# Attention and a maxout feed-forward on one core: regrouping the half-array matmuls of two pairs of heads into one turn

## The chip, the cores and the metric

The kernel runs on one core of one Trainium2 chip. The metric is the time of one execution on the device, in microseconds (us); the time shown for a kernel is the median of several executions. A profile is taken of one further execution; its span runs from the first to the last instruction on the core, and a little time lies around it.

## The reference: what is computed

Eight batches, twelve heads, sequence 448, head dimension 64. Attention with a softmax that has one more term in its denominator, then a feed-forward block whose hidden layer is the largest of three projections:

```python
scores = (1 / sqrt(64)) * q @ k.T                    # per batch and head: 448 x 448
e = exp(scores - m)                                  # m: row maximum
attn = e / (sum(e) + exp(-m) + 1e-09)                # the same as exp(s) / (sum(exp(s)) + 1)
x = (attn @ v), heads side by side                   # 3584 tokens x 768
h = max(max(x @ w1, x @ w2), x @ w3)                 # 768 -> 768
out = h @ w_out                                      # 768 -> 768, float32
```

## The kernel before, in words

**Pairs and engines.** Heads are handled two at a time: a *pair* p is two heads, six pairs make a batch, 48 pairs in all (NP = 48, NPAIR = 6). The sequence of 448 keys is cut into three chunks of 128 and a last one of 64. Matmul inputs are fp16. TensorE (PE) does all products; ScalarE (ACT) does the exponentials and the reciprocals (as Ln, L298, and Exp of minus it, L299); VectorE (DVE) casts q and k, normalizes, and empties the accumulators of the feed-forward part; GpSimd (POOL) scales v into fp16 (`scale_v`); SyncE (SP) issues the loads, the DMA transposes of q and k, and the stores.

**What is done for a pair.** `cast_qk` (L178 to L189) turns the loaded q and k into fp16 on DVE; `transposes` puts them head dimension first, from pair 12 (P_DMA) on by a DMA transpose on SP's queue (L209). `scores(p, c)` (L239) multiplies chunk c of the keys with all queries, one matmul for each head. The contraction is only 64 long, so each of these two matmuls uses one half of the array (64*128 in the profile) and the two run side by side. `exp_scores` (L249) takes both heads in one ACT instruction. `scores_last` (L255) does the last 64 keys of both heads in one matmul over the full array, and `exp_last` (L265) its Exp. `av_main(p, hh)` (L273) multiplies the three chunks of one head with v, with columns of ones beside v, so that the sums of the softmax come out of the same accumulator: three full-array matmuls. `av_last` (L285) adds the last 64 keys, one half-array matmul for each head. `reciprocals` does two Ln (one for each head) and one Exp on ACT, and `normalize(p, hh)` (L307) multiplies on DVE and so writes the input xT of the feed-forward part.

**Accumulators.** All of PSUM is given out: `ps_s` has two tiles of two banks for scores, `ps_av` two banks, one for each head of a pair (tag av), and `ps_u` two banks for the groups. A new tile takes the place of the one two before it in its pool, and its first matmul waits until that one has been read for the last time: by the Exp for scores, by `normalize` for av, by the eviction on DVE for a group.

**Groups.** The feed-forward part of a finished batch is cut into *groups*, kept in a queue and put between the steps of the next pairs to fill PE's time. An up group (L356) is six matmuls of 448 columns, evicted by DVE at L370 (first of three projections) or L372 (maximum with the others). An out group (op, L390) is six matmuls of 384 columns, evicted at L400; two of them fill a row tile, which is then stored. A batch has 18 up groups and then 6 or 8 out groups. `batch_done(b)` puts them in the queue when the last pair of the batch is normalized, and `n_groups` spreads them over the turns, leaving four (LEFT) for the start of the next batch.

**The order around the change.** The order on each engine is written out by hand (`manual_schedule`): every engine takes its instructions in the order of the program. One iteration `it` of the main loop holds the scores of pair `it` and the attention products of the pair before (`prev`). From pair 7 on:

```python
for c in range(2): exp_scores(p, c, scores(p, c))      # half array
group()
avs = [av_main(prev, hh) for hh in range(2)]           # full array
av_last(prev, avs)                                     # half array
stp = scores(p, 2)                                     # half array
stl = scores_last(p)                                   # full array
rb = reciprocals(prev, avs); exp_scores(p, 2, stp); exp_last(p, stl)
group(); normalize(prev, 0, avs, rb)
group(); normalize(prev, 1, avs, rb)
for _ in range(n_groups - 3): group()
```

From iteration 11 on the casts and the transpose of pair it + 2 and the scaling of v of pair it + 1 stand ahead of this, and the loads of pair it + 5 behind it. A run of half-array matmuls between full-array ones is called a stretch below; an iteration has two of them.

Of the kernel before, what the change touches and what calls it, by code (L numbers as in the profile page):

```python
# [21 lines left out]
def kernel(  # L22
# [20 lines left out]
    NPAIR = H // 2  # L43
    NP = B * NPAIR
# [79 lines left out]
    P_DMA = 2 * NPAIR  # L124
# [26 lines left out]
    qkTs = {}  # L151
# [13 lines left out]
    def cast_qk(p):  # L165
        qt, kt, _ = raw[(p // HB) % NRAW]
        h0 = 2 * (p % HB)
        hs = slice(h0, h0 + 2)
        k6, q6 = k16[p % NK], q16[p % NK]
        if p == 0:  # L170

            nc.scalar.copy(out=k6[:, 0:NB], in_=kt[:, hs, 0:NB].rearrange("p h c d -> p c h d"))
            for eng, cs in ((nc.scalar.copy, slice(0, 2)), (nc.vector.tensor_copy, slice(2, NB + 1))):
                eng(out=q6[:, cs], in_=qt[:, hs, cs].rearrange("p h c d -> p c h d"))
        else:
            if p >= P_DMA and (p // NPAIR) % 2:

                nc.vector.tensor_copy(  # L178
                    out=q6[:, 1 : NB + 1], in_=qt[:, hs, 0:NB].rearrange("p h c d -> p c h d")
                )  # L180
                nc.vector.tensor_copy(out=q6[64:128, 0], in_=qt[0:64, hs, NB])
            else:
                nc.vector.tensor_copy(out=q6, in_=qt[:, hs].rearrange("p h c d -> p c h d"))
            nc.vector.tensor_copy(  # L184
                out=k6[:, 0:NB], in_=kt[:, hs, 0:NB].rearrange("p h c d -> p c h d")
            )
        for hh, half in enumerate(halves):
            last = nc.gpsimd if p == 0 else nc.vector
            last.tensor_copy(out=k6[half, NB, hh], in_=kt[0:64, h0 + hh, NB])  # L189

    def scale_v(p):
        vt = raw[(p // HB) % NRAW][2]
        h0 = 2 * (p % HB)
        hs = slice(h0, h0 + 2)
        vs = vst[:, p % VB]
        scaled(
            vs[:, 0 : 2 * NB, D : 2 * D].rearrange("p (h c) d -> p h c d", h=2),
            vt[:, hs, 0:NB],
        )
        for hh, half in enumerate(halves):  # L200
            out_v = vlast[half, p % VB, hh] if p < NPAIR else vs[half, 2 * NB, D : 2 * D]
            scaled(out_v, vt[0:64, h0 + hh, NB])
# [32 lines left out]
    def scores(p, c):  # L235
        qkT, q0, k0 = qkTs[p]
        stp = ps_s.tile([128, 2, 512], FP32, tag="s", name="stp")
        for hh in range(2):
            nc.tensor.matmul(  # L239
                out=stp[:, hh, 0:S],  # L240
                lhsT=qkT[hh * D : hh * D + D, k0 + c * 128 : k0 + c * 128 + 128],
                rhs=qkT[hh * D : hh * D + D, q0 : q0 + S],
                start=True,
                stop=True,
            )
        return stp

    def exp_scores(p, c, stp):
        nc.scalar.activation(out=eT[:, p % 2, c], in_=stp[:, :, 0:S], func=AF.Exp, scale=scale)  # L249

    def scores_last(p):

        stl = ps_s.tile([128, 2, 512], FP32, tag="s", name="stl")
        qkT, q0, k0 = qkTs.pop(p)
        nc.tensor.matmul(  # L255
            out=stl[:, 0, 0:S],
            lhsT=qkT[:, k0 + NB * 128 : k0 + NB * 128 + 128],
            rhs=qkT[:, q0 : q0 + S],
            start=True,
            stop=True,  # L260
        )
        return stl
# [166 lines left out]
    def group():  # L429
        if queue:  # L430
            queue.pop(0)()

    LEFT = 4
    keep_busy(13)
    casts(0)
    transposes(0)
    keep_busy(3)
    for it in range(NP + 1):
        p = it if it < NP else None
        prev = it - 1 if it > 0 else None  # L440
        to_next = NPAIR - it % NPAIR
        n_groups = -(-max(len(queue) - LEFT, 0) // to_next) if it % NPAIR else 4
        n_groups = max(3, min(5, n_groups))

        first = {3: 1, 4: 2}.get(it)
        if first is not None:
            hs = slice(2 * first, 2 * first + 2)
            nc.vector.memset(raw[2][0][64:128, hs, NB - 1 : NB + 1, :], 0.0)
            if first == 1:
                load(NPAIR, 1, "v")  # L450
            load(NPAIR + first, 1)
        if it in (3, 4):
            load_weight(0, it - 3)
        if it in (5, 6, 8):
            load_weight((5, 6, 8).index(it) + 1)
        if it < NPAIR:

            casts(it + 1)
            for c in range(2):
                exp_scores(p, c, scores(p, c))  # L460
            if prev is None:
                keep_busy(3)
                exp_scores(p, 2, scores(p, 2))
                transposes(1)
                exp_last(p, scores_last(p))
            else:
                den, av = (ps_av.tile([128, 512], FP32, tag="av", name=n) for n in ("den", "av"))
                sums_main(prev, den, 1)
                stp = scores(p, 2)
                sums_main(prev, av, 0)  # L470
                stl = scores_last(p)
                sums_last(prev, den, 1)
                sums_last(prev, av, 0)
                exp_scores(p, 2, stp)
                exp_last(p, stl)
                rb = reciprocals_one(den)
                transposes(it + 1)
            if it < NPAIR - 1:
                keep_busy(3)
            else:  # L480

                ups = [up_open()]
                up_part(ups[0], 0, 0, 0, range(3))
                av5 = ps_s.tile([128, 2, 512], FP32, tag="s", name="av5")
                sums_main(p, av5[:, 1], 1)
                sums_main(p, av5[:, 0], 0)
                sums_last(p, av5[:, 1], 1)
                sums_last(p, av5[:, 0], 0)
                rb5 = reciprocals_one(av5[:, 1])
            if prev is not None:  # L490
                normalize_one(prev, av, rb)
            if it == NPAIR - 1:
                normalize_one(p, av5[:, 0], rb5)
                batch_done(0)
        elif it == NPAIR:
            exp_scores(p, 0, scores(p, 0))

            up_part(ups[0], 0, 0, 0, (3,))
            ups.append(up_open())
            up_part(ups[1], 0, 0, 1, range(4))  # L500
            ups.append(up_open(ps_av, "av"))
            up_part(ups[2], 0, 0, 2, range(4))
            for dc in (4, 5):
                for fc, ps in enumerate(ups):
                    up_part(ps, 0, 0, fc, (dc,))
                    if dc == 5:
                        up_close(ps, 0, 0, fc)
            del queue[0:3]
            exp_scores(p, 1, scores(p, 1))
            group()  # L510
            casts(it + 1)
            exp_scores(p, 2, scores(p, 2))
            exp_last(p, scores_last(p))
            group()
            transposes(it + 1)
            group()
        else:
            late = it + 1 < P_DMA
            if not late:

                if it + 2 < NP:
                    cast_qk(it + 2)
                    transposes(it + 2)
                if it + 1 < NP:
                    scale_v(it + 1)
            if p is not None:
                for c in range(2):
                    exp_scores(p, c, scores(p, c))
            group()
            if late:  # L530
                casts(it + 1)
            avs = [av_main(prev, hh) for hh in range(2)]
            av_last(prev, avs)
            if p is not None:
                stp = scores(p, 2)
                stl = scores_last(p)
            rb = reciprocals(prev, avs)
            if p is not None:
                exp_scores(p, 2, stp)
                exp_last(p, stl)  # L540
            if late:
                transposes(it + 1)
            group()
            normalize(prev, 0, avs, rb)
            group()
            normalize(prev, 1, avs, rb)
            if it % NPAIR == 0:
                batch_done(prev // NPAIR)
            if it + 2 == P_DMA:
                cast_qk(it + 2)  # L550
                transposes(it + 2)
            for _ in range(n_groups - 3):
                group()

        for n in range(NPAIR + HB, 2 * NPAIR) if it == NPAIR else (it + 5,):
            if it >= NPAIR and n < NP:
                load(n, 1)
    while queue:
        group()


# [1 line left out]
_INS = ['q', 'k', 'v', 'moe_w1', 'moe_w2', 'moe_w3', 'moe_w_out']  # L563
# [26 lines left out]
```

## Time and profile before

| | us |
|---|---|
| median of 3 executions | 368.15 (368.03 to 368.56) |
| the profiled execution | 367.77 |
| its span | 366.0 |
| PE busy / DVE busy / ACT busy | 357.3 / 243.7 / 220.6 |
| mean granted clock of TensorE | 0.996 |

How to read it. A row of the timeline gives the start and the length of some instructions merged into one, the engine, the line of the kernel, the operation, the tile written and the tiles read, the shape, and how many. Where the engine was idle before, the idle time and what ended it stand in brackets. PEld are the weight loads, which run beside the matmuls of PE. The length of a matmul is longer than its share of PE's time, since the next starts before it has ended; what a matmul costs is the distance from its start to the next one's start. L numbers are lines of the kernel before; up to L251 and from there to L420 the changed kernel has the same ones.

### The profile page before, as it was taken

To read this page: it belongs to the slowest core of one execution; us is meant where nothing else is said; L and a number is where in the kernel's file an instruction comes from. 1 tells how busy PE (TensorE), PEld (TensorE's weight loads), DVE (VectorE), ACT (ScalarE), POOL (GpSimd) and SP (SyncE) were. 2 spreads that over 40 slices of the span, in tenths; PEclk is the share of its full clock that TensorE was granted. 3 is DMA by queue.
4 is the path that set the end of the run, shared out by engine and by line. 5 is a ranking of instruction groups with operands and counts; after the bars stand their busy time and mean duration, and the time that the engine had idled before them with its cause. 6 is when DMAs were issued, how large, how long until landed. Compare 5 with 4: busy or idle time off the path is not lost.

```text
span 366.0 us, 6114 instructions
## 1 busy us (share of the span) xinstructions
PE 357.3 (98%) x2086; PEld 163.7 (45%) x2086; DVE 243.7 (67%) x521; ACT 220.6 (60%) x334; POOL 54.0 (15%) x159
## 2 busy tenths in 40 slices
PE   8999999999999999999999999999999999999994
PEld 3434444444444444444444444444444444445552
DVE  4564777876578677577657867757676876655553
ACT  4986476765666766666566676666566766651000
POOL 4263112211211211211121121121112112000000
PEclk9999999999999999999999999999999999999998
DMA  5999997668877879939764887847775673004006
GB/s 151 228 238 231 232 243 194 167 174 214 169 183 174 209 186 131 220 101 199 181 167 119 179 213 177 159 124 211 172 174 131 162 203 84 0 7 125 2 0 172
DMA packets 87792, 58.61 MB, mean 160 GB/s; under 512 B 43473, under 2 KB 84177, under 8 KB 87761
## 3 DMA queue, kind: packets, MB, share of 16 engines
q1 hardware_dynamic: 83552, 53.27, 60.7%
q0 software_dynamic: 3920, 4.72, 7.4%
q8 instruction: 16, 0.26, 0.3%
q10 hardware_dynamic: 288, 0.23, 0.2%
q14 instruction: 16, 0.12, 0.1%
HBM read 42.47 MB, written 11.01 MB: 146 GB/s over the span
## 4 chain that ended last, share of the span: by engine, by line
PE 94%; DVE 2%; ACT 1%; DMA 1%; issue 0%; SPq 0%; DVEq 0%
PE up L356 45%; PE op L390 15%; PE av L273 13%; PE stp L239 9%; PE stl L255 4%; PE av L285 3%; PE av L316 1%; DMA qin<-in_q_dram 1%; ACT eT L249 1%; PE trT L226 1%; PE trT L221 1%; DVE qkT L233 1%; DVE o_sb L400 0%; PE av L325 0%; PE busy L349 0%
## 5 line engine op out<-in xcount | busy, mean ns | idle before, releaser
L356 PE MATMUL up<-xT,w 128*128 128x448 f16 x864 | 175.3, 353 | 0.7 <-DVE xT L307 0.4
L249 ACT ACTIVATE eT<-stp 128x896 f16<-128x896 f32 x144 | 125.5, 910 | 53.9 <-PE stp L239 53.8
L356 PEld LDWEIGHTS <-w 128*128 128x128 f16 x864 | 81.6, 98 | 81.7 <-issue 12.5
L372 DVE TENSOR_TENSOR hT<-hT,up 128x448 f16<-128x448 f16 x96 | 59.6, 621 | 52.0 <-PE up L356 51.1
L157 POOL TENSOR_SCALAR vst<-vin 128x384 f16<-128x384 f32 x132 | 43.2, 338 | 255.1 <-issue 173.6
L298 ACT ACTIVATE lnd<-av 64x448 f32<-64x448 f32 x84 | 45.2, 538 | 48.9 <-PE av L285 47.9
L390 PE MATMUL op<-w,hT 128*128 128x384 f16 x336 | 59.3, 327 | 0.0
L273 PE MATMUL av<-eT,vst 128*128 128x448 f16 x252 | 54.5, 353 | 0.0
L307 DVE TENSOR_TENSOR xT<-av,rb 64x448 f16<-64x448 f32 x84 | 51.8, 617 | 1.4
L239 PE MATMUL stp<-qkT 64*128 64x448 f16 x288 | 44.1, 353 | 1.5 <-DVE qkT L233 0.7
L370 DVE CAST hT<-up 128x448 f16<-128x448 f32 x48 | 29.8, 624 | 22.9 <-PE up L356 22.2
L400 DVE TENSOR_SCALAR o_sb<-op 128x384 f32<-128x384 f32 x56 | 31.0, 553 | 20.0 <-PE op L390 19.0
L390 PEld LDWEIGHTS <-hT 128*128 128x128 f16 x336 | 31.6, 98 | 24.7 <-issue 4.0
L273 PEld LDWEIGHTS <-vst 128*128 128x128 f16 x252 | 24.6, 98 | 22.5
L184 DVE CAST qk<-kin 128x384 f16<-128x384 f32 x47 | 25.8, 549 | 1.8 <-DMA kin<-in_k_dram 1.4
L265 ACT ACTIVATE eL<-stl 128x448 f16<-128x448 f32 x48 | 25.9, 539 | 0.0
L299 ACT ACTIVATE rb<-lnd 128x448 f32<-128x448 f32 x42 | 24.2, 576 | 1.3
L239 PEld LDWEIGHTS <-qkT 64*128 64x128 f16 x288 | 11.0, 94 | 23.2 <-issue 16.8
L189 DVE CAST qk<-kin 64x64 f16<-64x64 f32 x94 | 17.9, 191 | 1.3
L255 PE MATMUL stl<-qkT 128*128 128x448 f16 x48 | 17.4, 363 | 0.0
L285 PE MATMUL av<-eL,vst 64*128 64x448 f16 x84 | 15.3, 360 | 0.0
L233 DVE COPY qkT<-trT 128x960 f16<-128x960 f16 x11 | 7.2, 656 | 9.9 <-PE trT L226 9.9
(49 smaller groups left out, 110.0 us busy)
## 6 DMA issues: line engine op xcount, KB each, us to landing
out_dram<-o_sb SPq DMA_DIRECT2D x56, 192.0 KB, 2.7
qin<-in_q_dram SPq DMA_DIRECT2D x46, 128.0 KB, 3.0
kin<-in_k_dram SPq DMA_DIRECT2D x45, 128.0 KB, 2.9
vin<-in_v_dram SPq DMA_DIRECT2D x44, 128.0 KB, 3.0
kin<-in_k_dram SPq DMA_DIRECT2D x46, 96.0 KB, 2.7
qin<-in_q_dram SPq DMA_DIRECT2D x45, 96.0 KB, 2.7
vin<-in_v_dram SPq DMA_DIRECT2D x44, 96.0 KB, 2.9
w<-in_moe_w_dram POOLq DMA_DIRECT2D x2, 1152.0 KB, 17.2
```

The lines of the kernel that those rows point to most:

```text
L157: nc.gpsimd.tensor_scalar(out=out, in0=in_, scalar1=LAMBDA, scalar2=1.0, op0=ALU.mult, op1=ALU.mult)
L239: nc.tensor.matmul(out=stp[:, hh, 0:S], lhsT=qkT[hh * D : hh * D + D, k0 + c * 128 : k0 + c * 128 + 128], rhs=qkT[hh * D : hh * D + D, q0 ...
L249: nc.scalar.activation(out=eT[:, p % 2, c], in_=stp[:, :, 0:S], func=AF.Exp, scale=scale)
L255: nc.tensor.matmul(out=stl[:, 0, 0:S], lhsT=qkT[:, k0 + NB * 128 : k0 + NB * 128 + 128], rhs=qkT[:, q0 : q0 + S], start=True, stop=True,)
L273: nc.tensor.matmul(out=av[:, 0:S], lhsT=vst[:, p % VB, hh * NB + c, (1 - hh) * D : (3 - hh) * D], rhs=eT[:, p % 2, c, hh, :], start=(c == ...
L298: nc.scalar.activation(out=lnd[mine], in_=avs[hh][other, 0:S], func=AF.Ln, bias=1.0)
L307: nc.vector.tensor_tensor(out=xTs[b][mine, j, :], in0=avs[hh][mine, 0:S], in1=rb[mine], op=ALU.mult)
L356: nc.tensor.matmul(out=ps[:, 0:S], lhsT=w_sb[i][:, dc, ts(fc, 128)], rhs=xTs[b][:, dc, :], start=(dc == 0), stop=(dc == NDC - 1),)
L370: nc.vector.tensor_copy(out=h, in_=ps[:, 0:S])
L372: nc.vector.tensor_tensor(out=h, in0=h, in1=ps[:, 0:S], op=ALU.max)
L390: nc.tensor.matmul(out=ps[:, 0:NW], lhsT=hTs[sb][:, fc, ts(t, 128)], rhs=wout_sb[:, fc, ts(nh, NW)], start=(fc == 0), stop=(fc == NFC - 1),)
L400: nc.vector.tensor_scalar(out=o_sb[:, ts(nh, NW)], in0=ps[:, 0:NW], scalar1=1.0 / LAMBDA, scalar2=None, op0=ALU.mult,)
```

## The change

From pair 12 on, the loop over single pairs is replaced by a loop whose turn holds two pairs, p and p + 1. The old loop ends at iteration 11, and av_main of pair 11 follows it. In a turn the half-array matmuls stand in three stretches: scores 0 and 1 of p with av_last of p - 1; score 2 of p with score 0 of p + 1; scores 1 and 2 of p + 1 with av_last of p. `scores_last` and `av_main` stand apart from them, among the groups. av_main of p + 1 stands at the end of the turn, behind `finish` of p. A turn takes eight groups where a batch begins and otherwise at least six, as many as share out what is queued. `prepare` (casts, transpose, scaling of v) and `load_next` come twice in a turn, for one pair each. The sizes of the pools stay. The rest of the diff names what was there before.

```diff
     def scores_last(p):
         stl = ps_s.tile([128, 2, 512], FP32, tag="s", name="stl")
-        qkT, q0, k0 = qkTs.pop(p)
+        qkT, q0, k0 = qkTs[p]
...
+    def prepare(p):
+        if p < NP:
+            cast_qk(p)
+            transposes(p)
+        if p - 1 < NP:
+            scale_v(p - 1)
+
+    def load_next(p):
+        if p < NP:
+            load(p, 1)
...
-    for it in range(NP + 1):
-        p = it if it < NP else None
+    for it in range(P_DMA):
+        p = it
...
+    def finish(prev, avs, rb, between=0):
+        for _ in range(between):
+            group()
+        normalize(prev, 0, avs, rb)
+        group()
+        normalize(prev, 1, avs, rb)
+        if prev % NPAIR == NPAIR - 1:
+            batch_done(prev // NPAIR)
+
+    avs = [av_main(P_DMA - 1, hh) for hh in range(2)]
+    for p in range(P_DMA, NP, 2):
+        left = max(len(queue) - LEFT, 0)
+        to_next = (NPAIR - p % NPAIR) // 2
+        n_groups = 8 if p % NPAIR == 0 else max(6, -(-left // to_next))
+        prepare(p + 2)
+        stps = [scores(p, c) for c in range(2)]
+        av_last(p - 1, avs)
+        for c in range(2):
+            exp_scores(p, c, stps[c])
+        group()
+        exp_last(p, scores_last(p))
+        rb = reciprocals(p - 1, avs)
+        finish(p - 1, avs, rb, 1)
+        stps = [scores(p, 2), scores(p + 1, 0)]
+        exp_scores(p, 2, stps[0])
+        exp_scores(p + 1, 0, stps[1])
+        prepare(p + 3)
+        load_next(p + 5)
+        for _ in range(n_groups - 7):
+            group()
+        avs = [av_main(p, hh) for hh in range(2)]
+        stps = [scores(p + 1, c) for c in (1, 2)]
+        av_last(p, avs)
+        for c in (1, 2):
+            exp_scores(p + 1, c, stps[c - 1])
+        rb = reciprocals(p, avs)
+        group()
+        exp_last(p + 1, scores_last(p + 1))
+        finish(p, avs, rb, 2)
+        load_next(p + 6)
+        avs = [av_main(p + 1, hh) for hh in range(2)]
+    av_last(NP - 1, avs)
+    rb = reciprocals(NP - 1, avs)
+    finish(NP - 1, avs, rb, 2)
     while queue:
         group()
```

More of the change, by code (lines that the diff above doesn't have):

```diff
@@ L519 @@
             if not late:
[L521 to L528, printed above, removed]
+                prepare(it + 2)
+            for c in range(2):
+                exp_scores(p, c, scores(p, c))
             group()
@@ L533 @@
             av_last(prev, avs)
-            if p is not None:
-                stp = scores(p, 2)
-                stl = scores_last(p)
+            stp = scores(p, 2)
+            stl = scores_last(p)
             rb = reciprocals(prev, avs)
-            if p is not None:
-                exp_scores(p, 2, stp)
-                exp_last(p, stl)
+            exp_scores(p, 2, stp)
+            exp_last(p, stl)
             if late:
@@ L546 @@
             normalize(prev, 1, avs, rb)
-            if it % NPAIR == 0:
-                batch_done(prev // NPAIR)
             if it + 2 == P_DMA:
@@ L557 @@
                 load(n, 1)
+    def finish(prev, avs, rb, between=0):
[14 more added lines that the diff above has]
+        av_last(p - 1, avs)
+        for c in range(2):
+            exp_scores(p, c, stps[c])
[24 more added lines that the diff above has]
+    finish(NP - 1, avs, rb, 2)
     while queue:
```

## The prediction

> **What bounds the kernel now.** I read the page's totals first, then the chain that ended last, then a stretch of steady turns by engine, then the waits of PE, and last the timeline around one turn.
>
> ```profile
> span 366.0 us, 6114 instructions
> PE 357.3 (98%) x2086; PEld 163.7 (45%) x2086; DVE 243.7 (67%) x521; ACT 220.6 (60%) x334; POOL 54.0 (15%) x159
> PE 94%; DVE 2%; ACT 1%; DMA 1%; issue 0%; SPq 0%; DVEq 0%
> ```
>
> PE sets the time. From 85 to 300 us it is busy for 215.00 of 215.00 us at clock 1.00, and its waits after 80 us add up to one line of 0.4 us:
>
> ```profile
> 85.00:300.00 215.00, 215.00 (x1222) 97.14 (x1221) 152.60 (x326) 140.76 (x214) 28.46 (x90) 1.00 0.74 174
> PE up L356 <- DVE xT L307: 0.4, 1, 0.4
> ```
>
> So a nanosecond of PE order saved is saved from the end, and a new wait of PE is paid in full: there is no slack to absorb it. The timeline of PE over one turn (start, length, line, instructions merged):
>
> ```profile
> 172.33 0.55 PE L239 MATMUL stp<-qkT 64*128 64x448 f16 x4
> 172.81 1.31 PE L356 MATMUL up<-xT,w 128*128 128x448 f16 x6
> 173.96 1.30 PE L273 MATMUL av<-eT,vst 128*128 128x448 f16 x6
> 175.19 0.36 PE L285 MATMUL av<-eL,vst 64*128 64x448 f16 x2
> 175.39 0.35 PE L239 MATMUL stp<-qkT 64*128 64x448 f16 x2
> 175.68 0.36 PE L255 MATMUL stl<-qkT 128*128 128x448 f16 x1
> ```
>
> Lengths overlap, so read start to start. Six full matmuls (64*128 is a half array, 128*128 a full one) go by in 1.15 us, 0.19 each. Six full ones ahead of a half pair take 173.96 to 175.19, 1.23: entering a stretch costs 0.09. Half pair to half pair is 0.20 (175.19 to 175.39); half pair to full is 0.29 (175.39 to 175.68): leaving costs 0.09. **One stretch costs 0.18 us** beyond its own matmuls. The op group that starts at 195.09 hands over at 196.07: 0.98 us, 0.163 each.
>
> **The saving.** Before, pairs 12 to 47 have two stretches each and the last iteration one: 73. After, 18 turns have three and the tail one: 55. Eighteen go: 18 x 0.18 = **-3.3 us**. Matmul counts are unchanged. (The Trainium skill, "TensorE: Matmul & The Clock Gate", section Back-to-back issue gap with the phases ahead of it, lets the drain of one matmul hide under the next; by it a removed stretch saves nothing and the sum is 3.3 us higher. "TensorEngine Tiling (Array Packing)", Key Properties, says that a change of mode drains the array; the steps of 0.29 beside 0.20 side with that page.)
>
> **The new wait.** Before, av_main(prev) comes after the next pair's first scores and a whole group, so the two av banks were freed long before. After, it stands at the end of the turn, directly behind `finish`: group, group, normalize 0, group, normalize 1, av_main(p+1). ps_av has two banks, both still hold pair p, and the changed program's order makes the first weight load of head 1 wait for DVE's normalize 1, which DVE can only start once it has evicted the third group. Before shows exactly this DVE chain, with nobody waiting on it:
>
> ```profile
> 167.69 4.70 PE L356 MATMUL up<-xT,w 128*128 128x448 f16 x24
> 169.03 0.62 DVE L370 CAST hT<-up 128x448 f16<-128x448 f32 x1 [2.05 <-PE up L356]
> 169.57 0.60 DVE L307 TENSOR_TENSOR xT<-av,rb 64x448 f16<-64x448 f32 x1
> 170.17 0.62 DVE L370 CAST hT<-up 128x448 f16<-128x448 f32 x1
> 170.82 0.63 DVE L307 TENSOR_TENSOR xT<-av,rb 64x448 f16<-64x448 f32 x1
> ```
>
> Call S the start of a group's last matmul. The second group there has S = 167.69 + 11 x 0.19 = 169.78; its eviction starts at S + 0.39, and normalize 1 ends at 171.45, S + 1.67. A weight load that waits for DVE starts 0.05 later and its matmul 0.06 (copy ending 23.42, load and matmul below):
>
> ```profile
> 22.76 0.66 DVE L233 COPY qkT<-trT 128x960 f16<-128x960 f16 x1 [0.32 <-PE trT L226]
> 23.47 0.11 PEld L239 LDWEIGHTS <-qkT 64*128 64x128 f16 x4 [0.62 <-DVE qkT L233]
> ```
>
> So head 1 starts at S + 1.73. Unhindered it would start at S + 0.19 + 3 x 0.19 = S + 0.76: **0.97 us lost per turn** (part may show at head 0, which needs normalize 0 and the same DVE). Behind op groups the same reading (groups from 197.99, S = 199.79, normalize 1 from 200.74 for 0.63) gives S + 1.64 against S + 0.73: 0.91. Everything on PE is queued behind that load: head 1, the next stretch, all groups. Each batch has two turns ending in up groups and one in op groups: 12 x 0.97 + 6 x 0.91 = 17.1. The same happens once more where the old loop hands over: av_main(11) follows normalize 1 of pair 10 with no group between (the queue leaves three there): + 0.9. Sum **+18.0**. By the quickest rows (eviction to normalize 0.48) it is about 0.8 each, 15; by the slowest (0.66, and normalize 0 pushing the third eviction by 0.15) about 1.2, 22. I take the chain as it stands.
>
> **The other av_main**, for pair p, has stretch B and n_groups - 7 groups between. Normalize 1 of p-1 waits there for the reciprocals: from the stretch's start, second Exp 1.22 (two take 172.74 to 174.47, overlapping), eL 2.05, two Ln and rb ending near 4.3 (steps 0.56, 0.57, 0.58), then normalize 0, an eviction and normalize 1, over at 6.1 to 6.3. Head 1 is due, from the same start: 0.68 for the stretch (0.20 + 0.20 + 0.28), a group, 0.20 for stl, two groups, 0.09 to enter stretch B, 0.48 for its two pairs, one group, three matmuls 0.57. With groups of 1.14 that is 6.58, no wait; with op groups of 0.98 (first turn of a batch, where only one group stands between) 5.94: 0.2 lost, five times, 0.9. In turn 12 group 4 is already the first up group of the new batch and needs the same normalize 1: 0.8 instead of the 0.4 of before. Together **+1.3**, with 0 and 4 as ends (nothing, or 0.2 in all 18).
>
> **Costed at nothing.** Scores: each tile reuses the one two back; the tightest, stl of p, comes 1.66 to 1.81 us after the turn's first scores, whose Exp ends at 1.31. Without that cover, up to 0.3 a turn. Casts (1.2 to 1.7 us of DVE) sit behind normalize 1; the group bank that they delay is due 0.3 later. Transposes go on SP behind a wait for the casts, with stores and loads behind them; two transposes (1.25), twelve loads (0.6) and up to eight stores are 9.7 to 14.5 us of issue in a turn of 15, and both transposes and loads are due a turn later, landing in 3. V scaling: 1.03 us on an engine 15% busy, due half a turn later or more. ACT has some 10 us in a turn of 15.
>
> **Sum.** -3.3 + 18.0 + 1.3 = +16.0. The profiled execution is 367.77 us (span 366.0 and 1.77 around it), 0.38 under the median of 368.15: 383.8 from the one, 384.1 from the other. I say 384.0.
>
> **Rivals.**
> *The bank is free in time* (faster). Place: the same weight load; it would need normalize 1 done before PE is three matmuls into av_main, or another bank. Below 3.3 / 19 = 0.17 us of wait a turn the change wins; with none it takes 364.5. For it: DVE is only 67% busy. Against: the order of DVE's queue, and 1.67 us of chain against 0.76. 0.05.
> *The wait is partly covered*: normalize 1 overlapping the eviction, or head 0 absorbing some, 0.3 to 0.6 a turn: 371 to 377. The rows of DVE show overlaps of 0.1 only. 0.08.
> *More falls late*: the first half's normalize in every turn (18 x 0.2 more), evictions behind casts (18 x 0.3), or SP's queue. 390 to 395. DVE's margins of 0.3 speak for it, SP's spare turn against. 0.08.
> *A stretch saves nothing*, all else as said: 387. The 0.29 beside 0.20 is against it. 0.03. (This is what the back-to-back rule of the Trainium skill's TensorE page would give.)
> That the change doesn't regroup the stretches is excluded by the program's order: it has three to a turn.
>
> **Chances.** Forecast 0.76. Range 377 to 391: it takes in the forecast with its bounds (-3.3 + 15 + 0 gives 379.5, -3.3 + 22 + 4 gives 390.5), and 387; about 0.18 is left out. About 0.2% (0.7 us) is what a measurement can tell from no change. Faster 0.05, the same 0.01, slower 0.94.
>
> **What the next profile would show.** Right: a PE wait at av L273 for DVE xT L307, some 19 times, about 1 us each over its loads and matmuls, 18 us in all, once per 15 us; PE no longer busy throughout; steps of 0.29 only three times a turn. The saving is wrong if the steps at the stretches' borders shrink or grow. The forecast fails if that wait is absent or under 0.5, or if PE waits elsewhere as well: at up for DVE hT, at stp for ACT eT or a transpose.

## The result, and the profile after

| | before | after |
|---|---|---|
| median, us (same chip) | 368.36 (368.03 to 368.57, 4 runs) | 383.36 (383.25 to 383.70, 4 runs) |
| ratio | | 1.0413 (95% interval 1.0401 to 1.0426) |
| profiled execution / span | 367.77 / 366.0 | 383.25 / 381.5 |

The change makes the kernel 15.0 us slower. The forecast was 384.0 in a range of 377 to 391.

The page's totals and the first line of its chain, of the kernel after:

```profile
span 381.5 us, 6140 instructions
PE 361.0 (95%) x2086; PEld 164.9 (43%) x2086; DVE 249.0 (65%) x521; ACT 224.2 (59%) x334; POOL 55.5 (15%) x159
PE 69%; SPq 9%; DMA 9%; DVE 7%; issue 4%; ACT 1%; DVEq 0%
```

PE still has 2086 matmuls, but it is no longer busy throughout. The waits of PE and of its weight loads (what waited, for whom, us in total, times, longest), of the kernel after:

```profile
PE av L273 <- DVE xT L307: 10.6, 25, 0.6
```
```profile
PEld L273 <- DVE xT L307: 20.1, 24, 1.0
```

The first is the line that the prediction named. Its total is less than what is lost, because PE counts as busy until the modelled end of the matmul before, and the weight loads' total is more, because a load is normally issued well ahead. What is lost has to be read from start to start, at one place. The end of a turn that closes with up groups, PE and then DVE, of the kernel after:

```profile
173.46 3.57 PE L356 MATMUL up<-xT,w 128*128 128x448 f16 x18
177.13 0.73 PE L273 MATMUL av<-eT,vst 128*128 128x448 f16 x3
178.41 0.74 PE L273 MATMUL av<-eT,vst 128*128 128x448 f16 x3 [0.55 <-DVE xT L307]
```
```profile
176.47 0.60 DVE L307 TENSOR_TENSOR xT<-av,rb 64x448 f16<-64x448 f32 x1
177.06 0.63 DVE L370 CAST hT<-up 128x448 f16<-128x448 f32 x1
177.72 0.63 DVE L307 TENSOR_TENSOR xT<-av,rb 64x448 f16<-64x448 f32 x1
```

The third group's last matmul starts at 173.46 + 17 x 0.19 = 176.69; that is S. Head 0 of av_main starts at 177.13, which is S + 0.44 and not S + 0.19: it waits for normalize 0 (176.47 + 0.60 = 177.07, and 0.06 more). Head 1 starts at 178.41, S + 1.72: normalize 1 ends at 178.35. Unhindered it would have been S + 0.76, so **0.96 us** are lost in this turn (0.98 with the step unrounded, 0.189), 0.25 of them at head 0.

A caution on the chain: it gives SP and DMA 9% each, through the casts. Yet the casts of k on DVE waited 0.7 us in all for loads:

```profile
DVE qk L184 <- DMA kin<-in_k_dram: 0.7, 2, 0.4
```

The chain follows back from each step to what released it last, even where that was long done. The experiments e1 and e7 below move 10 and 17 us without touching a transfer.

### The profile page after: what moved, and what is told of

Read it like the earlier page. It is cut to its first block, busy times and chain, and to the rows that moved or that the text cites. A ratio compares the mean times of both kernels' runs of the same rounds, so it can differ in the third digit from the quotient of the medians.

```text
span 381.5 us, 6140 instructions
## 1 busy us (share of the span) xinstructions
PE 361.0 (95%) x2086; PEld 164.9 (43%) x2086; DVE 249.0 (65%) x521; ACT 224.2 (59%) x334; POOL 55.5 (15%) x159
## 4 chain that ended last, share of the span: by engine, by line
PE 69%; SPq 9%; DMA 9%; DVE 7%; issue 4%; ACT 1%; DVEq 0%
PE up L356 35%; PE av L273 11%; PE op L390 10%; PE stp L239 8%; DMA kin<-in_k_dram 7%; DVE xT L307 5%; SPq L92 4%; SPq L93 3%; PE av L285 2%; PE stl L255 2%; SPq L209 1%; DVE hT L370 1%; DVE o_sb L400 1%; DMA out_dram<-o_sb 1%; DMA qin<-in_q_dram 1%
## 5 line engine op out<-in xcount | busy, mean ns | idle before, releaser
L249 ACT ACTIVATE eT<-stp 128x896 f16<-128x896 f32 x144 | 124.2, 914 | 102.0 <-PE stp L239 102.0
L356 PE MATMUL up<-xT,w 128*128 128x448 f16 x864 | 177.4, 353 | 0.8 <-DVE xT L307 0.4
L356 PEld LDWEIGHTS <-w 128*128 128x128 f16 x864 | 80.6, 98 | 86.4 <-issue 17.2
L157 POOL TENSOR_SCALAR vst<-vin 128x384 f16<-128x384 f32 x132 | 45.1, 343 | 266.3 <-issue 155.3
L273 PE MATMUL av<-eT,vst 128*128 128x448 f16 x252 | 58.6, 353 | 12.0 <-DVE xT L307 10.6
L390 PE MATMUL op<-w,hT 128*128 128x384 f16 x336 | 60.3, 327 | 0.1
L239 PE MATMUL stp<-qkT 64*128 64x448 f16 x288 | 41.3, 354 | 1.5 <-DVE qkT L233 0.7
L273 PEld LDWEIGHTS <-vst 128*128 128x128 f16 x252 | 22.6, 97 | 44.2 <-DVE xT L307 20.1
L189 DVE CAST qk<-kin 64x64 f16<-64x64 f32 x94 | 21.4, 228 | 1.3
L239 PEld LDWEIGHTS <-qkT 64*128 64x128 f16 x288 | 9.4, 94 | 29.5 <-issue 23.5
## 6 DMA issues: line engine op xcount, KB each, us to landing
w<-in_moe_w_dram POOLq DMA_DIRECT2D x2, 1152.0 KB, 17.2
```

The costliest lines, as they stand in the source:

```text
L157: nc.gpsimd.tensor_scalar(out=out, in0=in_, scalar1=LAMBDA, scalar2=1.0, op0=ALU.mult, op1=ALU.mult)
L239: nc.tensor.matmul(out=stp[:, hh, 0:S], lhsT=qkT[hh * D : hh * D + D, k0 + c * 128 : k0 + c * 128 + 128], rhs=qkT[hh * D : hh * D + D, q0 ...
L273: nc.tensor.matmul(out=av[:, 0:S], lhsT=vst[:, p % VB, hh * NB + c, (1 - hh) * D : (3 - hh) * D], rhs=eT[:, p % 2, c, hh, :], start=(c == ...
L356: nc.tensor.matmul(out=ps[:, 0:S], lhsT=w_sb[i][:, dc, ts(fc, 128)], rhs=xTs[b][:, dc, :], start=(dc == 0), stop=(dc == NDC - 1),)
L390: nc.tensor.matmul(out=ps[:, 0:NW], lhsT=hTs[sb][:, fc, ts(t, 128)], rhs=wout_sb[:, fc, ts(nh, NW)], start=(fc == 0), stop=(fc == NFC - 1),)
```

## The experiments

The theory: PE stands at av_main of p + 1 until DVE has freed the two av banks, and the length of the stop is DVE's queue (the third group's eviction, then normalize 1) against the three matmuls that PE can do meanwhile. The rivals: the stop is TensorE's own, from the new order; the stop comes from something else that ends then; fewer stretches gain nothing.

**e1: normalize 1 taken out from behind the third eviction.**

```diff
-        finish(p, avs, rb, 2)
+        group()
+        group()
+        normalize(p, 0, avs, rb)
+        normalize(p, 1, avs, rb)
+        if p % NPAIR == NPAIR - 1:
+            batch_done(p // NPAIR)
+        group()
```

> The changed kernel with one line moved: at the end of a turn normalize 1 stands directly behind normalize 0, ahead of the third group. Theory (PE waits at av_main for the av banks, and the length of the wait is the length of DVE's queue ahead of normalize 1): normalize 1 no longer stands behind the third group's eviction, so it ends about S + 1.1 us instead of S + 1.67 (S: start of the third group's last matmul); head 0 still waits 0.35, head 1 hardly. Wait per turn 0.4 instead of 0.95, 18 turns: -10 us, about 373. Rival (the stop comes from where av_main stands, or from something else that ends at that time, not from DVE's order): no change, 383. Rival (the eviction, now last, makes a later group wait for its bank instead): 383 again, with the wait at up and op.

Measured: 373.33 us (373.08 to 373.69), 1.0141 times the kernel before (1.0128 to 1.0155), 10.0 less than after. The same two places, of e1:

```profile
170.61 3.57 PE L356 MATMUL up<-xT,w 128*128 128x448 f16 x18
174.28 1.41 PE L273 MATMUL av<-eT,vst 128*128 128x448 f16 x6
175.62 0.55 PE L239 MATMUL stp<-qkT 64*128 64x448 f16 x4
```
```profile
173.62 1.26 DVE L307 TENSOR_TENSOR xT<-av,rb 64x448 f16<-64x448 f32 x2
```

S is 170.61 + 17 x 0.19 = 173.84; head 0 starts at S + 0.44 as before the move, but the six matmuls of av_main now last 175.62 - 174.28 = 1.34 where 1.23 is undisturbed: 0.25 + 0.11 = 0.36 lost, and no more. Behind op groups 0.46 are lost, so that 12 x 0.36 + 6 x 0.46 = 7.1 of the 17.2 us of the 18 turns stay and 10.1 go, as measured. The matmuls and their order on PE are those of the changed kernel; only DVE's order moved. So the stop is not TensorE's own, and it is the queue on DVE that makes its length.

**e2: one group put between normalize 1 and av_main.**

```diff
-        finish(p, avs, rb, 2)
+        finish(p, avs, rb, 1)
         load_next(p + 6)
+        group()
         avs = [av_main(p + 1, hh) for hh in range(2)]
```

> The changed kernel with the second finish of a turn given one group less ahead of it, and that group put between normalize 1 and av_main of p + 1. The three stretches stay. Theory (wait for the bank, 0.95 us a turn, hidden by 1.14 or 0.98 us of group): the 18 waits of 0.95 go, 17.2 us, to 366.2; in the turns that end in op groups normalize 0 now stands closer to the reciprocals and some 0.2 may stay, six times, so 366 to 367.6: below the kernel before. Rival (what was gained by fewer stretches is nothing, and the wait goes): 369.5. Rival (the wait only moves to the reciprocals): 375 or more, with DVE waiting for ACT at normalize 0 and PE at av.

Measured: 367.03 us (366.77 to 367.19), 0.9970 times the kernel before (0.9958 to 0.9981). The turn's end of e2:

```profile
167.95 3.57 PE L356 MATMUL up<-xT,w 128*128 128x448 f16 x18
171.36 1.30 PE L273 MATMUL av<-eT,vst 128*128 128x448 f16 x6
172.59 0.55 PE L239 MATMUL stp<-qkT 64*128 64x448 f16 x4
```

av_main starts 18 x 0.19 after the groups and lasts 1.23: nothing is lost. For TensorE the order of the matmuls is again that of the changed kernel, three groups and then av_main; what moved is where DVE's two multiplies stand among the evictions, each one group earlier. With the wait hidden, the three stretches are below the kernel before, if by little. What stays, read from start to start over the whole trace: 0.14 to 0.33 in three of the six turns that close with op groups (0.8 in all), 0.19 at the other av_main five times, 0.9 where the old loop hands over. The 0.8 is what stands between 367.0 and the 366.2 that a full cover was to give.

**e3 and e7: five, then ten matmuls over zeros put into the gap.** They add work and compute nothing that is used.

```diff
         load_next(p + 6)
+        keep_busy(5)
         avs = [av_main(p + 1, hh) for hh in range(2)]
```

> The changed kernel with five further matmuls over zeros (448 columns, full array, read by nobody) between finish and av_main of p + 1: 90 matmuls more, 18 x 5 x 0.19 = 17 us of TensorE work. Theory (PE stands idle there for 0.95 us a turn): they fit into the wait, the time stays within 1 us of 383.4. Rival (the time at av_main is TensorE's own, for the order or the change of mode): 400.

> The changed kernel with ten matmuls over zeros, in place of the five of e3, between finish and av_main of p + 1: 18 x 10 x 0.19 = 34.2 us of TensorE work. Theory (a wait of 0.97 behind up groups and 0.91 behind op groups, 17.2 in all): what doesn't fit is paid, 34.2 - 17.2 = 17.0, 400.4. Rival (the wait moves along with the work on TensorE, since DVE or ACT are held up as well): 417.

Measured: 383.93 us (383.45 to 384.43) with five, 400.29 us (400.01 to 400.51) with ten. The groups of these matmuls in the two traces, five and then ten to a turn (34 of them stand in the first iterations of either):

```profile
L349 PE MATMUL busy<-idle 128*128 128x448 f16 x124 | 29.4, 369 | 1.2 <-DVE idle L110 1.2
```
```profile
L349 PE MATMUL busy<-idle 128*128 128x448 f16 x214 | 47.0, 366 | 1.2 <-DVE idle L110 1.2
```

Ninety matmuls more, 17 us of TensorE work, cost 0.6 us, which the intervals of the two kernels (1.0414 to 1.0443 here, 1.0401 to 1.0426 for the change alone) don't tell from nothing; the next ninety cost 16.4. In the traces, from start to start, the first ninety lengthen the ends of the 18 turns by 0.1 us in all; another 0.46 is there before the first of these turns ends, in the part that the two kernels share (the second head of av_main of pair 11 starts at 75.05 in e3, at 74.59 in the changed kernel). The gap that the change opened holds about 0.95 us a turn, and beyond it PE's work is paid in full again.

**e4: the price of a stretch, on the kernel before.**

```diff
             av_last(prev, avs)
             if p is not None:
+                group()
                 stp = scores(p, 2)
...
-            group()
+            if p is None:
+                group()
             normalize(prev, 0, avs, rb)
```

> The kernel before with one of the groups that stood behind the scores moved between av_last and score 2 of iterations 7 to 47: the second stretch falls into two, 41 stretches more, the same matmuls. Theory (a stretch costs 0.18 us beyond its matmuls): + 7.5 us, 375.9, with PE never idle. Rival (entering and leaving is hidden under the neighbours): 368.4, no change. More than 378 would mean that score 2, now later, makes something wait.

Measured: 376.49 us (376.36 to 376.82), 8.4 more than before, ratio 1.0228 (1.0213 to 1.0244). From 85 to 300 us PE is busy for 215.00 of 215.00, so no new wait stands behind the 8.4. The stretch that was one and is now two, of e4:

```profile
170.97 0.36 PE L285 MATMUL av<-eL,vst 64*128 64x448 f16 x2
171.26 1.31 PE L356 MATMUL up<-xT,w 128*128 128x448 f16 x6
172.50 0.36 PE L239 MATMUL stp<-qkT 64*128 64x448 f16 x2
172.80 0.36 PE L255 MATMUL stl<-qkT 128*128 128x448 f16 x1
```

Each of the two leaves in 0.29 to 0.30 and the second is entered with 1.24 behind its group (1.14 undisturbed). 8.4 / 41 is 0.205 a stretch, a little more than the 0.18 expected: by the medians of start to start, a stretch of one pair leaves in 0.292 us, one of two pairs in 0.282, and here both halves are of one pair. 41 x (0.182 + 0.02) = 8.3. That a stretch is free is refuted.

What TensorE waits for at a border isn't shown. Two weight loads of the kernel before, beside the matmuls that the prediction shows:

```profile
173.77 1.04 PEld L273 LDWEIGHTS <-vst 128*128 128x128 f16 x6
175.19 0.10 PEld L285 LDWEIGHTS <-vst 64*128 64x128 f16 x2 [0.37 <-issue]
```

The loads of av_main start 0.19 ahead of their matmuls (173.77 against 173.96), but that of av_last starts with its matmul (both at 175.19). It is so at every border in the traces of before, after and e4. So the weight load, too, is held up there, and the runs don't separate what holds it.

**e5: e2 with the reciprocals of p ahead of the second Exp.**

```diff
-        for c in (1, 2):
-            exp_scores(p + 1, c, stps[c - 1])
-        rb = reciprocals(p, avs)
+        exp_scores(p + 1, 1, stps[0])
+        rb = reciprocals(p, avs)
+        exp_scores(p + 1, 2, stps[1])
         group()
```

> The kernel of e2 with reciprocals(p) put ahead of the Exp of score 2 of p + 1. In e2 three of the six turns that end in op groups still waited 0.14 to 0.33 us at av_main, with DVE idle until ACT's rb. Theory: rb now ends 0.8 us sooner, the wait at av_main at the turn's end goes wholly: 0.8 us less than e2, 366.2. Rival (the later Exp now makes av_main of p + 1 or the next scores wait): the same as e2 or more, with PE waiting for ACT eT.

Measured: 366.26 us (366.00 to 366.37), 0.9947 times the kernel before (0.9934 to 0.9959). No wait is left at the end of a turn; from start to start 1.84 us stay at L273 (five of 0.19, and the hand-over of 0.89).

**e6: two more covers.**

```diff
-        n_groups = 8 if p % NPAIR == 0 else max(6, -(-left // to_next))
+        n_groups = (9 if p // NPAIR % 2 == 0 else 8) if p % NPAIR == 0 else max(6, -(-left // to_next))
...
-            group()
-            normalize(prev, 0, avs, rb)
-            group()
-            normalize(prev, 1, avs, rb)
+            group()
+            if it + 1 < P_DMA:
+                normalize(prev, 0, avs, rb)
+                group()
+                normalize(prev, 1, avs, rb)
+            else:
+                for hh in range(2):
+                    normalize(prev, hh, avs, rb)
+                group()
```

> The kernel of e5 with two further covers: nine groups in the first turn of every other batch, so that two stand ahead of av_main of p, and in iteration 11 both normalizes ahead of the last group. Theory: of the waits left, the 0.19 at av_main of p goes in two turns, and the 0.9 where the old loop hands over falls to 0.3: 1.0 less than e5, 365.2. Rival (those waits are given back at the group banks or at the start of the next batch): 366.2.

Measured: 365.92 us (365.89 to 366.55), 0.9943 (0.9931 to 0.9956). This can't be told from e5. The waits aimed at did shrink, by 1.0 us at L273, but the trace shows most of it given back, as the rival has it. From start to start, two more out groups than in e5 wait 0.19 each for DVE's hT, and two up groups wait 0.13 each behind DVE's eviction: 0.6 together. And in turn 12, of e6:

```profile
80.57 0.36 PE L239 MATMUL stp<-qkT 64*128 64x448 f16 x2 [0.78 <-DMA qkT<-qk]
```

The transpose of pair 13 lands after score 0 of 13 wants it. From start to start that score is late by 0.9 us here, 0.7 in e3, 0.2 in e2 and in the changed kernel, and not at all in e5. The first up group of that turn waits for normalize 1 of pair 11 anyway, and the two losses add up to 0.80 or 0.81 in every one of these traces but e6, where they are 0.94. So the late score costs nothing in e3, and 0.13 in this run.

## Why the prediction was right, step by step

- *PE sets the time, a new wait is paid in full.* Right: the waits found, less what was saved, add up to the loss, below.
- *The wait at the end of a turn, 17.1 us.* Over the 18 turns the starts of av_main are late by 17.2 us: 0.95 to 0.98 behind up groups (0.97 forecast), 0.92 behind op groups (0.91 forecast). e1 and e2 take away what the mechanism says (10.0 and 16.3 us), e3 and e7 measure the gap from within. The chain on DVE could be read beforehand, because the kernel before runs the same sequence with nobody waiting for it.
- *The hand-over, 0.9.* 0.89, by av_main(11) at 73.30 and 74.59.
- *The other av_main, 1.3 together.* 0.19 in the five first turns of a batch (0.2 forecast). Turn 12 was mis-sized, by what the kernel before already lost. Its first up group waits 0.59 and the late score of pair 13 ahead of it 0.21, together the 0.8 forecast. But the kernel before lost 0.54 at that up group from start to start, not the 0.4 of the row of waits, and 0.27 at the scores of pair 12, which wait for nothing now. So + 0.06 at the up group and not + 0.4: 1.0 together (the two late scores, + 0.21 and - 0.27, nearly cancel and are left out).
- *The saving, 3.3.* The borders of a stretch are what they were, by the medians of start to start: 0.285 in and 0.282 out where 0.189 and 0.196 would be undisturbed. Two small gains were missed: scores_last behind a full matmul hands over in 0.189, not 0.199, and av_last behind scores takes 0.186, not 0.196, each 36 times, 0.7 in all. e4 shows from the other side that the price is real. So the page of the Trainium skill on TensorE ("TensorE: Matmul & The Clock Gate", the phases ahead of Back-to-back issue gap), by which neighbours hide each other's drain, fits full matmuls among themselves here (steps of 0.189, though the rows give each a modelled length of 0.353), and doesn't fit a change of mode, where the Trainium skill's "TensorEngine Tiling (Array Packing)", Key Properties, has the drain. e4 shows the price of the change of mode; that a drain is what costs it is that page's word and is not shown.
- *Costed at nothing.* Score banks, casts and V scaling made PE wait for nothing new. Transposes and loads had their spare turn, but for the transpose of pair 13 in turn 12. An out group that waits 0.19 for DVE's eviction at 115.35 is new and was not seen.
- Sum by the trace: -3.3 - 0.7 + 17.2 + 0.9 + 1.0 + 0.2 = 15.3, against 15.5 between the spans. Between the medians it is 15.0, since the profiled execution of the kernel before was quicker than all of its timed ones. The forecast's + 16.0 is 0.7 above the 15.3, by the small gains (0.7) and turn 12 (0.3) that it missed, less the out group (0.2) and 0.1 more of the large waits.

The rival on the other side needed less than 0.17 us of wait a turn. e2 and e5 bring the wait below that, and there the three stretches a turn do win: 1.0 and 1.8 us.

The Trainium skill's "Perfetto Trace Analysis", in Identifying Performance Opportunities, says that the same bubble coming back on the engine that should be saturated can mean too little SBUF or PSUM for the next tile. Here it came back once a turn, at a tile that wanted one of two banks, so the page points to the right place; but e2 removes it with the same two banks, by the order alone.

## What to carry to other kernels

When a producer is moved right behind the reader that frees its buffer, count the reader's whole queue from the moment at which the last thing ahead of it can start: here an eviction and a multiply, 1.7 us, against 0.76 us of work on the engine that waits. On an engine that is busy throughout, such a move can cost far more than the switches it saves (here 19 us against 4), and one independent block of work behind the reader hid it in e2. The chain can be read from the kernel before whenever it runs there without being waited for.

## What the runs showed of the hardware

- A half-array stretch costs 0.18 us beyond its matmuls (448 columns), and 0.01 more to leave when it holds one pair instead of two (0.292 against 0.282).
- Between the end of DVE's multiply and the start of the matmul that waits for it at av_main lie 0.05 to 0.06 us, in all 43 such waits of the changed kernel.
- Five full matmuls (0.945 us) put into a gap of 0.92 to 0.98 us lengthened the end of a turn by 0.02 us behind op groups and by less than 0.01 behind up groups (e3 against the changed kernel). TensorE's mean clock was 0.996 to 1.0 in all these runs, with and without the gaps of 1 us, so the gaps did not lower it.
